# Attention, expert routing and a dense FFN on one core: v as 128 rows, route counts behind the value product, w1 in eight pieces, w2's low products last, a last unit without conditions

## The chip, the core and the metric

The kernel runs on one core of a Trainium2 chip. A core has five engines, each with its own instruction stream: TensorE (PE in the profile, its weight loads PEld), VectorE (DVE), ScalarE (ACT), GpSimd (POOL) and SyncE (SP), which here only issues transfers. The transfers run on 16 DMA engines. The metric is the device time of one execution in microseconds (us); lower is better.

## The reference, cut to what matters

```python
# q, k, v: 8 batches, 8 heads, 576 positions, 64 wide
k_p = k.reshape(B, H, 72, 8, D).mean(axis=3)      # keys and values pooled by 8
v_p = v.reshape(B, H, 72, 8, D).mean(axis=3)
attn = softmax(q @ k_p.T / 8)
x = attn @ v_p                                    # 4608 tokens of 512
do_compute = x @ w_skip > 0                       # other tokens pass unchanged
e = argmax(x @ w_gate)                            # one of 8 experts, 512 -> 1024 -> 512
x = x + gate * (relu(x @ w1[e]) @ w2[e])          # for the tokens that compute
h = x @ w_in                                      # dense FFN, 512 -> 2048 -> 512
out = (h * sigmoid(h)) @ w_out
```

## The kernel before

**Attention** (`attention`, L173 to L418). 36 tiles of 128 tokens run in a software pipeline, i from -2 to 35: in a step PE makes the scores of tile i+2 (`s`, from the key tile `kbd` and `q`), the transposes of tile i+1's weights (`pt`) and the value product of tile i (`pv`, from `pts` and the value tile `vex`). VectorE takes the maxima (`mx`), ScalarE the exponentials (`prb`). The loads of k, q and v (`loadk`, `loadq`, `loadv`) are issued by SP a batch or two ahead, all on one queue. v comes as 120 rows of five chunks (600 places for 8 heads x 72 pooled values). It is pooled by GpSimd and for batch 0 in part by VectorE (L216), then transposed for a small product with the router's weights (`vtp`, `cps`), which fills further columns of `vex`.

**Routing** (`route`, L429). Tokens are routed in groups of 9, 9, 9, 6 and 3 tiles. Each group has steps that are hung between the attention's: `step1` makes a one-hot tile (`rohb`) on VectorE, `count` sums it on PE with two small 0/1 matrices (`trib`, `onesb`; `trib` is cast by `consts`, from the tile `constb`), `step2` makes each token's place (`ix`) on VectorE, and `place` (L529) has GpSimd scatter the tokens' numbers into a list in DRAM (`slots`), one operation of about 1 us per tile. At the end the list is read back as a table.

**Expert units** (`moe`, L794). A unit is up to 384 tokens of one expert. Products are made of three matmuls on parts: each operand is split into a high part (a cast, on ScalarE: `w1h`, `w2h`, `hh`, `xth`) and a low part (the rest, on VectorE: `w1l`, `w2l`, `hl`, `xtl`). `mm1` (L809) makes eight hidden groups f of 12 matmuls each (`hp`, three buffers), high x high, low x high, high x low over four chunks of 128. `mm2` (L847) makes the output for each third s of the unit, 24 matmuls over f (`yp`). `keep` (L805) copies the gathered tokens (`xn`) to `xr` for the residual. The first unit stands ahead of the loop; its weights come during attention (`expert0`, passed to `attention` as `extra`: `conv1` splits w1 chunk by chunk at i = 29 to 32, `xtrans` transposes tokens at i = 34 and 35). Then a `For_i` loop (L947) runs over the units; the hardware loads each unit's token count n and takes one of three versions of `mm1` by nested conditions (L958, L961), and skips thirds (L913). In a pass `second` (L891) has the output products, the scatters of the results to DRAM (which read the token numbers `si`), and the split of the next w1. The last unit stands behind the loop; its matmuls lie inside conditions on its count (L986, L1007), interleaved with the preparation of the FFN's weights.

**The FFN** (`ffn`, from L1105) follows; from about 545 us on it is almost all PE.

**Order.** Every engine runs its instructions in the order of the code (a recording layer, `Ordered`, L110, keeps it, so all these instructions carry line L110); a wait of one holds what stands behind it on its engine.

## Time and profile before

| | us |
|---|---|
| three runs | 1317.8, 1320.7, 1322.06 (median 1320.7) |
| the profiled execution | 1320.69 |
| its span in the trace | 1318.9 |
| PE busy | 1268.2 (96%) |
| VectorE busy | 854.9 (65%) |
| ScalarE busy | 569.1 (43%) |
| GpSimd busy | 354.4 (27%) |

Times in the trace count from the start of the span. The page gives busy shares, and groups of equal instructions with their number, busy time, mean duration and the idle time ahead of them; the timeline gives single instructions (or runs of equal ones, with x and their number) with their start, their duration, and in brackets how long their engine was idle before them and what ended that. A PE row for several matmuls gives the time from the first one's start to the last one's modelled end, so rows overlap a little. The windows view sums a stretch: busy time of each engine, the granted TensorE clock as a share of the full one, the busy share of the DMA engines and the bytes that they moved.

### The profile page before, as it was taken

How to read it: one execution, taken by the hardware profiler on the slowest of the kernel's cores; microseconds unless marked ns; L12 is line 12 of the kernel's file. 1: busy time of each engine (PE TensorE's matmuls, PEld its weight loads, DVE VectorE, ACT ScalarE, POOL GpSimd, SP SyncE). 2: the span in 40 equal slices, each digit the busy share in tenths (PEclk: the TensorE clock that was granted, in tenths of full speed). 3: DMA queues.
4: the chain of work that ended last, by engine and by line, in shares of the span. 5: the costliest groups of instructions: out<-in, count | busy, mean ns of one | idle time of the engine just before them, and what ended most of it. 6: DMA issues, size and time to landing. Idle time of an engine off the chain costs nothing.

```text
span 1318.9 us, 20479 instructions
## 1 busy us (share of the span) xinstructions
PE 1268.2 (96%) x6501; PEld 1081.3 (82%) x6502; DVE 854.9 (65%) x1554; ACT 569.1 (43%) x1188; POOL 354.4 (27%) x312
## 2 busy tenths in 40 slices
PE   5899789999989999999999999999999999999998
PEld 5788778988979888878888888788888888888887
DVE  4677786667667677779833325565784657847565
ACT  4567633454445454344433334433353333533321
POOL 4476332222123230223357603101011110101100
PEclk9999898999999999999999999999999999999999
DMA  9988635555556552248935332635356452463532
GB/s 287 291 261 256 213 132 195 191 188 192 179 197 210 195 191 83 89 160 271 319 115 211 137 121 88 217 126 176 109 189 205 153 175 90 166 203 132 175 107 93
DMA packets 94106, 233.77 MB, mean 177 GB/s; under 512 B 15068, under 2 KB 26972, under 8 KB 90375
## 3 DMA queue, kind: packets, MB, share of 16 engines
q1 hardware_dynamic: 86735, 215.82, 48.9%
q0 software_dynamic: 7008, 16.80, 3.9%
q8 instruction: 42, 0.69, 0.2%
q14 instruction: 33, 0.27, 0.1%
q10 hardware_dynamic: 288, 0.20, 0.1%
HBM read 182.58 MB, written 52.89 MB: 179 GB/s over the span
## 4 chain that ended last, share of the span: by engine, by line
PE 57%; DVE 2%; issue 1%; ACT 1%; DMA 0%; SPq 0%; DVEq 0%; ACTq 0%
PE yb L110 20%; PE ps L110 17%; PE fh L110 9%; PE fop L110 9%; PE yp L110 1%; PE hp L110 1%; DVE ft L110 1%; PE fxp L110 0%; DMA wout<-wdo 0%; DVE fr L110 0%; PE sx L110 0%; DVE fgl L110 0%; DVE fsg L110 0%; ACT fh L110 0%; DVE hl L110 0%
## 5 line engine op out<-in xcount | busy, mean ns | idle before, releaser
L110 PE MATMUL yb<-wout,g 128*128 128x512 f32 x1152 | 268.4, 391 | 0.7 <-DMA wout<-wdo 0.7
L110 PEld LDWEIGHTS yb<-wout,g 128*128 128x128 f32 x1152 | 215.0, 188 | 45.6 <-DMA wout<-wdo 1.1
L110 POOL TENSOR_TENSOR tm<-tm,tm 128x512 f32<-128x512 f32 x24 | 32.3, 1344 | 411.7 <-ACT tm L110 411.7
L110 DVE TENSOR_TENSOR yacc<-yb,yacc 128x512 f32<-128x512 f32 x168 | 116.0, 690 | 38.7 <-PE yb L110 31.4
L110 ACT COPY tm<-ps 128x512 f32<-128x512 f32 x72 | 42.3, 588 | 146.3 <-PE ps L110 144.5
L110 PE MATMUL yp<-w2h,hh 128*128 128x512 f32 x240 | 96.2, 401 | 1.7 <-ACT w2h L110 1.3
L110 PE MATMUL yp<-w2l,hh 128*128 128x512 f32 x240 | 94.3, 393 | 2.4 <-DVE w2l L110 2.4
L110 PE MATMUL yp<-w2h,hl 128*128 128x512 f32 x240 | 94.5, 394 | 0.0
L110 ACT ACTIVATE hh<-hp 128x256 fp32r<-128x256 f32 (+2 forms) x96 | 41.2, 429 | 122.4 <-PE hp L110 113.0
L110 ACT CAST g<-sg 128x512 fp32r<-128x512 f32 x96 | 59.6, 620 | 76.9 <-DVE sg L110 76.9
L110 DVE TENSOR_TENSOR fsg<-fh,fsg 128x512 f32<-128x512 f32 x48 | 33.0, 688 | 81.4 <-ACT fsg L110 81.4
L110 ACT ACTIVATE prb<-s,mx 128x72 f32<-128x72 f32 x288 | 65.2, 343 | 47.4 <-DVE mx L110 46.0
L110 PE MATMUL fh<-w1l,fh 128*128 128x512 f32 x336 | 83.4, 390 | 0.0
L110 DVE TENSOR_TENSOR tm<-ps,tm 128x512 f32<-128x512 f32 x24 | 16.6, 691 | 98.1 <-PE ps L110 98.1
L110 PE MATMUL hp<-xth,w1h 128*128 128x256 f32 (+2 forms) x384 | 72.3, 310 | 5.4 <-PEq L1573 2.3
L110 PE MATMUL hp<-xtl,w1h 128*128 128x256 f32 (+2 forms) x384 | 73.5, 311 | 3.6 <-DVE xtl L110 3.3
L110 DVE SCALAR_TENSOR_TENSOR hl<-hp,hh 128x256 fp32r<-128x256 f32 (+2 forms) x96 | 46.0, 479 | 42.8 <-ACT hh L110 39.5
L110 PEld LDWEIGHTS fh<-w1l,fh 128*128 128x128 f32 x336 | 62.8, 188 | 12.9
L110 PE MATMUL hp<-xth,w1l 128*128 128x256 f32 (+2 forms) x384 | 71.0, 307 | 0.0
L110 DVE TENSOR_TENSOR g<-sg,g 128x512 fp32r<-128x512 f32 x96 | 65.7, 685 | 5.1 <-ACT g L110 4.7
L110 PE MATMUL pv<-vex,pts 120*128 120x148 f32 (+3 forms) x400 | 63.6, 315 | 5.3 <-remote 2.7
L110 DVE TENSOR_TENSOR w2l<-raw,w2h 128x512 fp32r<-128x512 f32 x96 | 65.8, 690 | 3.3
(231 smaller groups left out, 2751.2 us busy)
## 6 DMA issues: line engine op xcount, KB each, us to landing
raw<-w SPq DMA_DIRECT2D x88, 512.0 KB, 3.3
wout<-wdo SPq DMA_DIRECT2D x48, 512.0 KB
win<-wdi SPq DMA_DIRECT2D x36, 512.0 KB
w1l<-wdi SPq DMA_DIRECT2D x36, 512.0 KB
xa<-x SPq DMA_DIRECT2D x36, 256.0 KB
fx<-xa SPq DMA_DIRECT2D x9, 1024.0 KB
v<-vR SPq DMA_DIRECT2D x7, 1200.0 KB
fr<-w_in SPq DMA_DIRECT2D x16, 512.0 KB
```

The source lines that it names most:

```text
L110: ins = f(*a, **k)
```

## The change

The change makes these edits:

- v is padded to 128 rows on the host and loaded as such (two pieces for batch 0, seven whole batches after it). The computation still reads 120.
- k of batch 0 comes in four loads, q's first tile in two, between them; its pooling and key tile are made in matching pieces. The constants are loaded ahead of the identity. For batch 1, q is loaded ahead of v.
- `count` is issued behind the value product of its step; `consts` at i = 8.
- `expert0` splits w1 in eight half chunks (512 columns) at i = 28 to 35; from i = 32 on the low part is made by GpSimd.
- `keep` is one copy on ScalarE.
- In the loop the version of `mm1` for 256 tokens stands first, the one for 384 last.
- `mm2` of the first unit's s = 2 takes the eight products with w2's low part behind the others.
- `si` is made behind the step s = 1 (in the loop that is behind w1's low parts).
- The last unit's count is no longer loaded, and its conditions are gone. (By construction the last unit holds 384 places or none.)

On SP, at the start of the program (`kT`, `qT`, `vR` are the inputs, the numbers behind names count tiles), before:

```order
L110 DMA k_121<-kT 128x1152 x2
L110 DMA q_126<-qT 128x4x128
L110 DMA v_129<-vR 120x1536
L110 DMA v_129<-vR 120x1024
L110 DMA q_126<-qT 128x4x448
L110 DMA wr<-wr 128x144
L110 DMA k_134<-kT 128x2304
L110 DMA v_178<-vR 120x2560
L110 DMA q_180<-qT 128x2304
```

and now:

```order
L110 DMA k_121<-kT 128x576 x2
L110 DMA q_122<-qT 128x2x128
L110 DMA k_121<-kT 128x576 x2
L110 DMA q_122<-qT 128x2x128
L110 DMA v_132<-vR 128x1536
L110 DMA v_132<-vR 128x1024
L110 DMA q_122<-qT 128x4x448
L110 DMA wr<-wr 128x144
L110 DMA k_137<-kT 128x2304
L110 DMA q_185<-qT 128x2304
L110 DMA v_187<-vR 128x2560
```

The k and q pieces alternate, v has 128 rows, and the whole q of batch 1 stands ahead of v.

On PE, near the end of attention, around the count of the fourth group (`rps`), before:

```order
L110 MATMUL pv_2147<-vex_113,pts_2073 128x3x74
L110 MATMUL pv_2147<-vex_113,pts_2073 128x2x74 x3
L110 LDWEIGHTS trib
L110 MATMUL rps_2183<-rohb_2164,trib 128x48
...
L110 MATMUL rps_2183<-rohb_2164,onesb 128x48
...
L110 MATMUL rps_2183<-rohb_2164,onesb 128x8
L110 MATMUL pt_2192<-ident,prb_116 120x128 x3
L110 MATMUL pt_2197<-ident,prb_116 120x128 x2
L110 MATMUL pv_2201<-vex_113,pts_2137 128x2x74
L110 MATMUL pv_2201<-vex_113,pts_2137 128x3x74
L110 MATMUL pv_2201<-vex_113,pts_2137 128x2x74 x3
```

and now:

```order
L110 MATMUL pv_2156<-vex_113,pts_2082 128x3x74
L110 MATMUL pv_2156<-vex_113,pts_2082 128x2x74 x3
L110 MATMUL pt_2195<-ident,prb_116 120x128 x3
L110 MATMUL pt_2200<-ident,prb_116 120x128 x2
L110 MATMUL pv_2204<-vex_113,pts_2146 128x2x74
L110 MATMUL pv_2204<-vex_113,pts_2146 128x3x74
L110 MATMUL pv_2204<-vex_113,pts_2146 128x2x74 x3
L110 LDWEIGHTS trib
L110 MATMUL rps_2210<-rohb_2173,trib 128x48
...
L110 MATMUL rps_2210<-rohb_2173,onesb 128x48
...
L110 MATMUL rps_2210<-rohb_2173,onesb 128x8
```

The count with `trib` and `onesb` has gone behind the transposes `pt` and the value product `pv` that it stood in front of.

On GpSimd, at the end of attention (`xn` is the gather of the first unit's tokens, `ix` the places that a scatter needs), before:

```order
L110 TENSOR_TENSOR vex_113<-vp_1684,consts 120x2x64 x3
L110 DMA slots<-consts,ix_1868 36864x1 x9
L110 DMA xn<-xa,g_85 128x520 x3
L110 DMA slots<-consts,ix_2228 36864x1 x6
L110 MEMSET pad_w_2308 128x1
```

and now:

```order
L110 TENSOR_TENSOR vex_113<-vp_1691,consts 120x2x64 x3
L110 DMA slots<-consts,ix_1875 36864x1 x9
L110 DMA xn<-xa,g_85 128x520 x3
L110 TENSOR_TENSOR w1l<-raw_79,w1h 128x512 x2
L110 DMA slots<-consts,ix_2239 36864x1 x5
L110 TENSOR_TENSOR w1l<-raw_79,w1h 128x512
L110 DMA slots<-consts,ix_2239 36864x1
L110 TENSOR_TENSOR w1l<-raw_79,w1h 128x512
L110 MEMSET pad_w_2323 128x1
L110 DMA slots<-consts,ix_2419 36864x1 x3
```

Four operations for w1's low part stand between the gather and the scatters; the third of them behind five scatters, the fourth behind all six.

The diff, cut to its core:

```diff
@@ loadv, pool_k, keys
-                    nc.sync.dma_start(v_t[b][:CP, c].rearrange("p c t d -> p c (t d)"), self.vR[b][:, c])
+                    nc.sync.dma_start(v_t[b][:, c].rearrange("p c t d -> p c (t d)"), self.vR[b][:, c])
...
+                for a in halves:
+                    eng.tensor_reduce(kp[:, a:a + w], k[:, a:a + w], AX.X, ALU.add)
...
-            def keys(b):
-                kp, kb = st.pop((b, "k")), kbd[b % NB]
-                for j in range(2):
-                    nc.scalar.mul(kb[:, :, j, :], kp, c[:, C_E + j:C_E + j + 1])
+            def keys(b, parts=(slice(4),)):
+                kp, kb = st[b, "k"], kbd[b % NB]
+                for a in parts:
+                    for j in range(2):
+                        nc.scalar.mul(kb[:, a, j, :], kp[:, a], c[:, C_E + j:C_E + j + 1])
@@ attention: start
-            for a in (0, 2):
-                nc.sync.dma_start(k_t[0][:, a:a + 2].rearrange("p a g t -> p a (g t)"), self.kT[0][:, a:a + 2])
+            q_t[0] = s2.tile([P, 4, S], F32, name="q0", tag="q", bufs=3)
+            for a in range(4):
+                nc.sync.dma_start(k_t[0][:, a].rearrange("p g t -> p (g t)"), self.kT[0][:, a])
+                if a % 2:
+                    nc.sync.dma_start(q_t[0][:, a - 1:a + 1, 0:P], self.qT[0][:, a - 1:a + 1, 0:P])
+            nc.scalar.dma_start(c, self.con[:, P:P + C_TRI])
             nc.scalar.dma_start(self.ident, self.con[:, 0:P])
...
-            pool_k(0, nc.vector)
-            keys(0)
+            pool_k(0, nc.vector, range(4), 1)
+            keys(0, (slice(0, 2), slice(2, 4)))
@@ attention: step i
-                if ready and ready[0]:
-                    ready[0]()
                 if i == -2:
                     pool_v(0, ON0)
                     values(0)
+                    loadq(1)
                     loadv(1)
-                    loadq(1)
...
                 if i >= 0:
                     pv(i, pts.pop(i))
+                if ready and ready[0]:
+                    ready[0]()
...
-                if i == 6:
+                if i == 8:
                     self.consts()
@@ conv1, keep
-    def conv1(self, i, eng=None):
-        self.split(self.w1h[:, i], self.w1l[:, i], self.raw1[:, i], eng=eng)
+    def conv1(self, i, eng=None, a=0, m=FM):
+        self.split(*[t[:, i, a:a + m] for t in (self.w1h, self.w1l, self.raw1)], eng=eng)
...
             def keep():
-                nc.scalar.copy(xr[:, U - 1], xn[:, U - 1])
-                nc.vector.tensor_copy(xr[:, 0:U - 1], xn[:, 0:U - 1])
+                nc.scalar.copy(xr.rearrange("p s n -> p (s n)"), xn.rearrange("p s n -> p (s n)"))
@@ mm2
-            def mm2(s, gt, between=None):
+            def mm2(s, gt, between=None, low_last=False):
...
+                a, b, c = (hh, self.w2h), (hh, self.w2l), (hl, self.w2h)
+                order = [(f, t) for f in range(8) for t in (a, b, c)]
+                if low_last:
+                    order = [(f, t) for f in range(8) for t in (a, c)][:-1]
+                    order += [(f, b) for f in range(4)] + [(7, c)] + [(f, b) for f in range(4, 8)]
@@ second
                     if n is None:
-                        mm2(s, gt)
+                        mm2(s, gt, low_last=(s == 2))
...
                     if s == 2:
                         scatter(s)
-                        nc.vector.tensor_scalar(si[:, 0:U - 1], cols[:, 0:U - 1], -1.0, None, ALU.add)
                         if n is not None:
                             self.conv1(0)
...
+                    else:
+                        nc.vector.tensor_scalar(si[:, 0:U - 1], cols[:, 0:U - 1], -1.0, None, ALU.add)
@@ loop
-            nq = nc.value(self.qi[0:1, 1:2], U * P)
...
-                with tc.If(n > 320) as cmp:
-                    mm1(384)
+                with tc.If(n < 257) as cmp:
+                    mm1(256)
                 with cmp.Else():
-                    with tc.If(n > 256) as cmp2:
+                    with tc.If(n < 321) as cmp2:
                         mm1(320)
                     with cmp2.Else():
-                        mm1(256)
+                        mm1(384)
@@ last unit
             for f in range(0, 8, 2):
-                with tc.If(n > 0) as cmp:
-                    nc.before(cmp)
-                    mm1(U * P, (f, f + 1))
-                nc.after(cmp)
+                mm1(U * P, (f, f + 1))
...
             for s in (2, 1):
-                with tc.If(n > P * s) as cmp:
-                    nc.before(cmp)
-                    mm2(s, gt)
-                nc.after(cmp)
+                mm2(s, gt)
@@ host, expert0
+    vr = np.concatenate([vr, np.zeros((B, P - CP, NC, POOL * D), v.dtype)], 1)
...
-                if 29 <= i < 33:
-                    k.conv1(i - 29)
+                if 28 <= i < 36:
+                    k.conv1((i - 28) // 2, k.nc.gpsimd if i >= 32 else None, FM // 2 * (i % 2), FM // 2)
```

## Rows read from the trace of the kernel before

**Rows 1.** of the page: the costliest groups (see the section on the profile), then DMA issues

```profile
L110 POOL TENSOR_TENSOR tm<-tm,tm 128x512 f32<-128x512 f32 x24 | 32.3, 1344 | 411.7 <-ACT tm L110 411.7
...
v<-vR SPq DMA_DIRECT2D x7, 1200.0 KB
```

**Rows 2.** the windows view: window, length, busy us (instructions) of each engine, clock, DMA share, GB/s

```profile
19.00:24.00 5.00, 5.00 (x29) 4.42 (x28) 2.96 (x9) 2.54 (x12) 0.00 (x0) 1.00 1.01 218
25.00:30.00 5.00, 3.83 (x27) 3.21 (x25) 4.79 (x13) 3.41 (x14) 3.99 (x2) 1.00 0.95 390
```

**Rows 3.** the timeline at startup: start, us, engine, operation, [idle before <- releaser]

```profile
8.24 0.96 ACT L110 ACTIVATE kbd<-kp,consts 128x288 f32<-128x288 f32 x2 [5.04 <-DVE kp L110]
...
9.25 2.29 PE L110 MATMUL s<-kbd,q 128*128 128x144 f32 x8 [9.25 <-ACT kbd L110]
...
11.95 2.76 DVE L110 TENSOR_REDUCE vp<-v 120x192 f32<-120x1536 f32 x1
...
14.03 2.06 POOL L110 TENSOR_TENSOR v<-v 120x512 f32<-120x512 f32 x2 [4.19 <-DMA v<-vR]
...
17.13 2.14 PE L110 MATMUL s<-kbd,q 128*128 128x144 f32 x8
...
28.60 1.25 PE L110 MATMUL s<-kbd,q 128*128 128x144 f32 x8 [1.02 <-DMA q<-qT]
```

**Rows 4.** the timeline at 52 to 57 us, ScalarE and TensorE

```profile
52.87 0.30 ACT L110 CAST trib<-constb 128x128 bf16<-128x128 f32 x1 [4.77 <-DMA constb<-con]
...
54.07 1.60 PE L110 MATMUL s<-kbd,q 128*128 128x144 f32 x8 [2.62 <-ACT prb L110]
...
56.44 3.85 PE L110 MATMUL pv<-vex,pts 120*64 120x148 f32 x20
```

**Rows 5.** the timeline at the end of attention

```profile
152.08 3.05 PE L110 MATMUL pv<-vex,pts 120*128 120x148 f32 x10 [2.69 <-remote]
...
162.33 1.30 DVE L110 TENSOR_TENSOR w1l<-raw,w1h 128x1024 fp32r<-128x1024 f32 x1 [0.71 <-ACT w1h L110]
...
165.73 0.18 PE L110 MATMUL rps<-rohb,trib 128*128 128x48 bf16 x1 [2.45 <-DVE rohb L110]
...
170.28 2.51 PE L110 MATMUL pv<-vex,pts 120*64 120x148 f32 x20 [0.91 <-DVE ri L110]
```

**Rows 6.** the timeline around the first unit's first group, GpSimd and TensorE

```profile
172.01 1.02 POOL L110 DMA_INDIRECT slots<-consts,ix  x1 [8.63 <-DVE sc L110]
...
176.37 0.85 PE L110 MATMUL hp<-xth,w1l 128*128 128x384 f32 x4
...
178.50 0.98 POOL L110 DMA_INDIRECT slots<-consts,ix  x1 [0.30 <-issue]
```

**Rows 7.** the timeline in the first unit's second product

```profile
195.80 0.70 DVE L110 COPY xr<-xn 128x1040 f32<-128x1040 f32 x1
...
196.89 2.53 DVE L110 TENSOR_TENSOR w2l<-raw,w2h 128x512 fp32r<-128x512 f32 x4
...
197.62 0.50 PE L110 MATMUL yp<-w2l,hh 128*128 128x512 f32 x1 [1.87 <-DVE w2l L110]
```

**Rows 8.** the timeline of TensorE in the loop's first pass

```profile
219.36 0.39 PE L110 MATMUL hp<-xth,w1h 128*128 128x256 f32 x1 [1.86 <-issue]
...
220.40 1.05 PE L110 MATMUL hp<-xth,w1l 128*128 128x256 f32 x4
...
224.38 0.62 PE L110 MATMUL hp<-xth,w1l 128*128 128x256 f32 x4
```

**Rows 9.** the view of tile hp in 210 to 506 us: forms of ScalarE's relu

```profile
L110 ACT ACTIVATE hh<-hp x80: 383/412/492, 217.3 to 486.1; 128x256 fp32r<-128x256 f32 x40, 128x320 fp32r<-128x320 f32 x32, 128x384 fp32r<-128x384 f32 x8
```

**Rows 10.** the timeline of the pass with the fewest tokens

```profile
385.43 0.17 DVE L110 TENSOR_SCALAR si<-table 128x2 int32 x1 [1.77 <-DMA xa<-x,si]
...
391.17 0.82 PE L110 MATMUL hp<-xtl,w1h 128*128 128x256 f32 x2 [2.39 <-DVE xtl L110]
```

**Rows 11.** the timeline of TensorE at the loop's exit

```profile
505.98 1.34 PE L110 MATMUL hp<-xth,w1h 128*128 128x384 f32 x4 [2.27 <-PEq L1573]
```

More of the change, by code (lines that the diff above doesn't have):

```diff
@@ L200, in loadq, with pool_k @@
                 nc.sync.dma_start(q_t[b], self.qT[b])
-            def pool_k(b, eng, halves=(0, 2)):
+            def pool_k(b, eng, halves=(0, 2), w=2):
                 k = k_t[b]
@@ L206, in pool_k @@
                     kp = s2.tile([P, 4, G], F32, name=f"kp_{b}", tag="kp")
-                if eng is nc.vector:
-                    for a in halves:
-                        eng.tensor_reduce(kp[:, a:a + 2], k[:, a:a + 2], AX.X, ALU.add)
-                else:
-                    eng.tensor_tensor(k[:, :, :, 0:4], k[:, :, :, 0:4], k[:, :, :, 4:8], ALU.add)
-                    eng.tensor_tensor(k[:, :, :, 0:2], k[:, :, :, 0:2], k[:, :, :, 2:4], ALU.add)
-                    eng.tensor_tensor(kp, k[:, :, :, 0], k[:, :, :, 1], ALU.add)
+                for a in halves:
+                    eng.tensor_reduce(kp[:, a:a + w], k[:, a:a + w], AX.X, ALU.add)
                 st[b, "k"] = kp
@@ L769, in moe_first @@
         self.sel, self.nu = [pool.tile([1, 1], I32, name=n, tag=n) for n in ("sel", "nu")]
-        self.qi = pool.tile([1, 2], I32, name="qi", tag="qi")
+        self.qi = pool.tile([1, 1], I32, name="qi", tag="qi")
         sq = pool.tile([P, U + 1], I32, name="sq", tag="sq")
@@ L845, in gates @@
                 return gt
-            def mm2(s, gt, between=None):
+            def mm2(s, gt, between=None, low_last=False):
                 ps = (pp if s else self.hp).tile([P, DM], F32, name=f"yp{s}", tag="yp" if s else "hp")
-                i = 0
-                for f in range(8):
-                    if between and f == 4:
+                a, b, c = (hh, self.w2h), (hh, self.w2l), (hl, self.w2h)
[3 more added lines that the diff above has]
+                    order += [(f, b) for f in range(4)] + [(7, c)] + [(f, b) for f in range(4, 8)]
+                for i, (f, (h, w)) in enumerate(order):
+                    if between and i == 12:
                         between()
-                    for h, w in ((hh, self.w2h), (hh, self.w2l), (hl, self.w2h)):
-                        nc.tensor.matmul(ps, h[:, f, P * s:P * (s + 1)], w[:, f], start=(i == 0), stop=(i == 23))
-                        i += 1
+                    nc.tensor.matmul(ps, h[:, f, P * s:P * (s + 1)], w[:, f], start=(i == 0), stop=(i == 23))
                 nc.vector.scalar_tensor_tensor(y[:, s, 0:DM], ps, gt[:, s:s + 1], xr[:, s, 0:DM], ALU.mult, ALU.add)
@@ L1513, in layout @@
     vr = np.concatenate([vr, np.zeros((B, NC * CP - H * G, POOL * D), v.dtype)], 1)
[L1514 removed]
+    vr = vr.reshape(B, NC, CP, POOL * D).transpose(0, 2, 1, 3)
+    vr = np.concatenate([vr, np.zeros((B, P - CP, NC, POOL * D), v.dtype)], 1)
     wr = np.concatenate([w_gate, w_skip[:, None]], 1).reshape(H, D, E + 1).transpose(1, 0, 2).reshape(D, H * (E + 1))
```

7 lines of the change are left out of this document (removed).

## The prediction

> **What bounds the kernel now.** I read the page first: TensorE (PE) is busy 96% of the span (the table ahead), so in most stages only a change in PE's own work or in its few waits can move the end. I then went through the stretches in order of time and looked in each at the places where PE waits, because the change leaves PE's matmuls as many and as large as they were. The last two thirds (the dense FFN from about 545 us on) hold no edited line; they only shift with their start. So the question is which of PE's waits before that go, and what is late next. The reader should see three kinds of wait in the rows: for loads (startup, and at 54 us), for VectorE or GpSimd work queued in a bad order (166, 197, 391 us), and for the sequencers at the loop's entry and exit (219, 506 us). Behind several of them PE then runs a stretch at the lower of its two clock levels: the 2.62 us wait at 54 us is followed by a value product of 20 matmuls that takes 3.85 us, where the same shape takes 2.51 later [rows 4, 5].
>
> The profiled execution took 1320.69 us, at the median of the three runs (1320.7), so gains are subtracted from it directly. A measurement of this kernel tells about 0.3%, 4 us, from no change.
>
> **Loads of v.** In the stretch 19 to 24 us, which is all v with its 120 rows, the queues are full (share 1.01) and move 218 GB/s; in 25 to 30 us, q and k with 128 rows, they are as full (0.95) and move 390 GB/s [rows 2]. A whole v is 1200 KB [rows 1], 1.23 MB; at 218 GB/s that is 5.6 us. With 128 rows it is 1.31 MB and at the rate of the other loads 3.4 us, so each of the eight loads gets 2.2 us shorter. I take that value since 128 rows is what k and q have; the other end is no gain.
>
> The Trainium skill ("DMA: Bandwidth & Descriptors", "Why a DMA increments its semaphore by 16 and not by 1") says that a transfer goes to the largest number of engines up to 16 that divides its slowest dimension, which is 15 for 120 rows and 16 for 128. By that rule each engine has 8 rows both ways, and v would take as long as before. The row speaks against it as the whole story, since 15 of 16 would cost 6% and the row shows 44% less. What it would give stands among the rivals.
>
> **Startup.** GpSimd waits 4.19 us for v until 14.03, VectorE begins its part of the pooled v at 11.95 and takes 2.76, and the transposes that need both stand ahead of the scores at 17.13 [rows 3]. With v 2.2 to 3 us earlier GpSimd's part comes that much earlier; then VectorE's is the later one. It begins behind the first scores' maxima, and so moves only as far as these. The key tile takes 0.96 us in one piece at 8.24 and the scores 2.29 from 9.25 [rows 3]; in halves, the first half of both (0.5 and 1.1 us) can be done before the second half of k is pooled, which is 1.6 at most. The scores at 17.13 come 1.2 us earlier if the halves bring nothing and 3.1 if both work; I take **2.5**. The constants ahead of the identity and the four smaller k loads I cost at nothing: the same bytes on the same queue.
>
> **q before v.** PE waits 1.02 us at 28.60 for q, which is queued behind v [rows 3]. It is now in front: **1.0**. v(1) is then one load of q later, which at the new rate lands about when it used to; at the old rate its transposes would wait about 2.
>
> **54 us.** ScalarE stands 4.77 us for the small constants, queued behind whole loads, and casts them only at 52.87; the exponentials and PE wait behind it, PE 2.62 [rows 4]. The cast moves two tiles later, and the queues are some 6 us ahead after three faster v. The wait should go, and of the 1.3 us by which the value product behind it was slow about half: **3.2**, bounds 1 and 3.9.
>
> **Count behind the value product, w1 in halves.** At 165.73 PE waits 2.45 for the route's one-hot tile [rows 5]. The work that it stands in front of (transposes of the next weights) could not have begun much earlier, because VectorE did 1.30 us of w1's low part at 162.33 ahead of the maxima. In the new order that piece is on GpSimd, and the count comes after the value product. I take **2.0** for this place; at the other three counts the wait was far shorter. VectorE's route steps behind a count start later by a value product, and so do the scatters of slots; GpSimd is idle 8.63 us before them [rows 6]. The 2.69 us wait at 152.08 [rows 5] is for value tiles which VectorE made late for a reason that I can't see in the trace; I count nothing for it, and 2.7 as the upper end.
>
> **The price: w1's low parts on GpSimd.** The third and fourth chunk's low parts now stand in GpSimd's queue among the slot scatters. The first half of the fourth chunk stands behind five scatters that wait for the route's index. Those start at 172.01 and follow each other at 1.30 us, so the fifth is over at 172.01 + 4 x 1.30 + 1.0 = 178.2; a GpSimd operation of 128 x 512 takes 1.34 us [rows 1]. The piece is there at about 179.8. The first unit's first group of matmuls needs it in its last product, the fourth of those at 176.37, so at 176.9 [rows 6]. PE stands 2.9 us. Since slow matmuls follow several of PE's longer waits [rows 4, 8, 11], I charge **-3.5**. Bounds: 0 (the index comes earlier because VectorE has less to do) and -4.6 (the wait and a whole slow stretch of 1.7, as at the loop's entry below). The second half, behind one more scatter, is needed four groups later and is covered.
>
> **First unit's second product.** PE waits 1.87 us at 197.62 for w2's low parts 4 to 7, which VectorE makes from 196.89 in 2.53 us [rows 7]. With the low products last, PE has 19 products that need none of them; the copy of xr (0.70 us) no longer stands ahead of them on VectorE [rows 7], so the last is there at 196.89 + 2.53 - 0.70 = 198.7, and the product can't end sooner. The wait goes; some of it may come back for the very last part, or a slow stretch behind it may go too: bounds 1.0 and 2.9, **1.8**.
>
> **Loop entry.** In the first pass PE stops 1.86 us at 219.36 with nothing to wait for that the trace shows, in the second group of the 256-token branch, which stands last in the code; the matmuls after it run at 1.05 us for four instead of 0.62 further on [rows 8]. In the four later passes of that size the row isn't there. I read it as the jump over the two longer branches while the weights of the pass are loading. With the 256 branch first the code runs on. Gain 0 to 3.6 (1.86 and four groups at 0.43 more): **1.9**.
>
> **si behind w1's low parts.** In the pass of fewest tokens VectorE waits 1.77 us at 385.43 until a scatter has read si, ahead of w1's four low parts, and PE waits 2.39 at 391.17 for what follows them [rows 10]. si moves behind: **1.7**; the rest of the 2.39 stays with the low parts themselves. Elsewhere in the loop it costs nothing, since the scatter that reads si is not waited for by PE.
>
> **xr in one copy.** VectorE's copy of two thirds takes 0.70 us [rows 7]; ScalarE's of the whole I put at up to 2, and it must now wait for VectorE's last read of xr. The first relu of a pass is some 1 us later then. The cover is the matmuls' three output buffers, that is two groups of three such rows as the 0.62 us one [rows 8]. So 0, and -2 if the cover fails in some passes.
>
> **Last unit without conditions.** The matmul at 505.98 waits 2.27 us at the loop's exit, and its four take 1.34 us, where four of this shape take 0.85 [rows 6, 11]. The barrier stays; a load of the count to a register and eight pairs of branches go. **1.2**, between 0.5 and 2.5.
>
> **Sum:** 2.5 + 1.0 + 3.2 + 2.0 - 3.5 + 1.8 + 1.9 + 1.7 + 1.2 = 11.8 us; 1320.7 - 11.8 = **1308.9 us**.
>
> **Rivals.** *v stays slow.* If what holds the rate is not the 120 rows (the rule above), startup gives 1 instead of 2.5, q before v loses 2 at v's transposes instead of 0, and of the 3.2 at 54 us half stays: 1.5 + 2 + 1.6 less, 1314 us. For it: the number of engines differs only by one. Against: in the rows two full queues differ by 390 to 218. *More than counted.* The wait at 152 us goes with the lighter VectorE (2.7), the slow stretches go with the waits before them, and GpSimd's pieces come in time: 8 more, 1301 us.
>
> *Slower.* The stop at 219 us may be the price of every jump past code that has not been fetched, and the new order would then move it behind the branch: the 256-token passes jump past two blocks at the end of theirs, the 320-token passes past one. The rows count five passes of 256 (40 groups of 8), four of 320 and one of 384 [rows 9]. Each stop costs 1.86 and a slow stretch of 1.7, some 3.5 us. Without the gain of 1.9 the kernel stands at 1310.8; four stops make 1324.8, from there on it is slower, and nine make 1342. Against it: in the present code later passes jump too, over 384 and 320 to the 256 branch, and don't stop; that is why I hold it for unlikely. If only the first pass stops, 1314.
>
> **How the numbers follow.** Forecast with its bounds, 1303 to 1313: 0.60. v stays slow: 0.12. One first stop, or GpSimd's price at its bound, 1313 to 1318: 0.10. More than counted: 0.13. Jumps: 0.05. The range takes in the first three and the better case down to 2 us beyond its value, and leaves out the jumps and the far ends: 1299 to 1318. Faster by over 0.3% (below 1316.7): the forecast, the better case, nearly all of the slow v and of the one stop, 0.60 + 0.13 + 0.10 + 0.04 = 0.87, less 0.02 for several costs at once: 0.85. Slower (above 1324.7), the jumps: 0.05. Within: 0.10.
>
> **What would show it.** Right: v windows at about 390 GB/s; scores (1) near 14.5; no wait near 51 us; no 2.45 us wait for the one-hot tile; a PE wait of about 3 us in the first unit's first group whose releaser is GpSimd's low part; no 1.87 wait for w2's low parts; no stop in the first pass. Wrong: v still near 218 GB/s, or "issue" waits on PE behind the branch in many passes, or a first-unit wait far above 5 us because the route's index came late.

## The result and the profile after

The changed kernel takes 1329.6 us (median of six runs, 1328.1 to 1331.9) against 1321.4 of the kernel before beside it: 1.0066 times as long, 95% interval 1.0045 to 1.0086. The forecast was 1308.9. The profiled execution's span is 1329.8 us (before 1318.9), and PE is busy 1272.4 us in it, 4 us more than before: the rest is waiting. In the experiments one execution, of run 12, took 7194 us where the other three took 1304.9 to 1307.5; it is left out.

To see where the time went, I compared the start of every PE matmul in the two traces. Negative numbers are us that the changed kernel is ahead of the one before, at that time of the old trace:

| time before | place | ahead (-) or behind (+) |
|---|---|---|
| 17 | end of the startup | -0.75 |
| 60 | behind the constants' cast | -5.5 |
| 107 | behind two counts | -1.5 |
| 160 | end of attention's tiles | +1.0 |
| 173, 181 | first unit's first groups | +3.7, +6.1 |
| 201 | first unit's second product | +3.1 |
| 215, 223 | loop, first and second groups | +8.8, +5.3 |
| 243 | loop, behind the first pass | +12.1 |
| 388, 394 | pass of fewest tokens | +13.0, +10.5 |
| 415 | the same, its end | +14.4 |
| 525 to the end | last unit, dense FFN | +11.1 |

So PE gains at 54 us, in the second product, at the loop's entry, in the pass of fewest tokens and at the last unit, and five stretches lose more than all that: 60 to 160, 160 to 181, 201 to 215, 223 to 243 and 394 to 415. The waits view of the changed kernel (engine, tile, releaser; us in total, times, longest) names most of them:

```profile
PE pv L110 <- DVE x L110: 7.6, 8, 2.8
PE xtp L110 <- DVE xtl L110: 6.2, 2, 3.3
PE pv L110 <- DVE vex L110: 4.3, 1, 4.3
...
PE xtp L110 <- issue: 3.2, 1, 3.2
PE hp L110 <- POOL w1l L110: 2.4, 1, 2.4
```

Only the last of these was in the prediction's sum. Two of the others stood in part in the kernel before, which waits 2.69 us for the same `pv` [rows 5] and 2.71 for one of the two `xtp`.

**Loads.** The windows view (columns as in [rows 2]) of the whole v and of the loads behind it:

```profile
18.00:23.00 5.00, 5.00 (x28) 4.42 (x27) 3.02 (x10) 2.45 (x11) 0.00 (x0) 1.00 1.01 424
24.00:28.00 4.00, 3.32 (x25) 2.89 (x23) 3.90 (x11) 2.40 (x10) 3.58 (x2) 1.00 1.00 420
```

128 rows take v from the 218 GB/s of [rows 2] to 424. Run 4 below, the kernel before with this part alone, shows the same in a stretch that is all v:

```profile
16.00:18.50 2.50, 2.50 (x12) 2.21 (x10) 0.91 (x2) 1.54 (x8) 0.64 (x2) 1.00 1.00 422
```

By the rule that the prediction quoted from the Trainium skill ("DMA: Bandwidth & Descriptors", "Why a DMA increments its semaphore by 16 and not by 1") an estimated 6% of the rate was to be had; the measurement decides, it was nearly a factor of two. The DMA view counts 66 packets of some 10 KB in 20 to 23 us of the kernel before, with the engines full, which is 0.74 us for each; in 20 to 22 us of the changed one 83 of them, 0.39 us each. Why a packet takes longer with 120 rows, no run shows. What the faster v did at startup stands in the timeline (start, us, engine, operation, [idle before <- releaser]), to be held against [rows 3]:

```profile
11.38 2.78 DVE L110 TENSOR_REDUCE vp<-v 120x192 f32<-120x1536 f32 x1 [0.23 <-DMA v<-vR]
...
13.28 2.06 POOL L110 TENSOR_TENSOR v<-v 120x512 f32<-120x512 f32 x2 [6.23 <-DMA v<-vR]
...
16.38 1.90 PE L110 MATMUL s<-kbd,q 128*128 128x144 f32 x7
```

GpSimd still waits for v, until 13.28 instead of 14.03. Run 4 below shows what the faster v alone does there.

**Counts.** VectorE and PE at the first count:

```profile
63.15 0.16 DVE L110 TENSOR_TENSOR tot<-tot,rps 128x8 f32<-128x8 f32 x1 [1.21 <-PE rps L110]
...
64.71 0.17 DVE L110 SCALAR_TENSOR_TENSOR ix<-pf,sl 128x9 int32<-128x9 f32 x1
64.80 0.16 DVE L110 TENSOR_SCALAR sm<-pv 128x8 f32<-128x8 f32 x1
...
66.11 1.66 PE L110 MATMUL pv<-vex,pts 120*128 120x148 f32 x10 [0.79 <-DVE x L110]
```

VectorE waits 1.21 us for the count (`rps`), which now comes behind the value product. It then does the nine route steps from `tot` to `ix`, and only after them the sums `sm` and the outputs `x` of the tile before, for which PE's next value product waits. This place costs 1.2 us, the next two counts 1.1 and 1.3. The other 2.8 us or so that are lost between 60 and 141 us go at two places without a count, where VectorE stands still for no reason that I found (see "Still open" below).

**GpSimd's pieces.** GpSimd, VectorE and PE in the last group's route and at the first unit's first group (timeline):

```profile
164.06 0.20 DVE L110 TENSOR_REDUCE rm<-req 128x6 f32<-128x48 f32 x1
164.30 1.88 DVE L110 TENSOR_TENSOR roh<-req,rm 128x48 f32<-128x48 f32 x1
...
164.82 2.60 POOL L110 TENSOR_TENSOR w1l<-raw,w1h 128x512 fp32r<-128x512 f32 x2
...
166.21 1.27 DVE L110 TENSOR_TENSOR rohb<-roh,rdo 128x48 bf16<-128x48 f32 x1
...
168.89 3.05 PE L110 MATMUL pv<-vex,pts 120*128 120x148 f32 x10 [2.79 <-DVE x L110]
...
181.51 1.28 POOL L110 TENSOR_TENSOR w1l<-raw,w1h 128x512 fp32r<-128x512 f32 x1
...
182.85 0.44 PE L110 MATMUL hp<-xth,w1l 128*128 128x384 f32 x1 [2.45 <-POOL w1l L110]
```

The two VectorE steps `roh` and `rohb` end with GpSimd's two pieces, at about 166.1 and 167.4. They last 1.88 and 1.27 us; without GpSimd beside them such steps take 0.21 (run 13 below). PE's next value product waits 2.79 us for what follows on VectorE. The Trainium skill ("GPSIMD Engine Reference", "1. Specifications") says that GpSimd shares its ways to SBUF with VectorE, and that VectorE's instructions with two SBUF inputs contend for them. The trace agrees and gives the price here: such a step lasts until the GpSimd instruction beside it ends. A step with one input from SBUF isn't slowed: VectorE's pooling of k takes 1.34 us beside GpSimd's work on v,

```profile
24.34 4.53 POOL L110 TENSOR_TENSOR v<-v 120x1280 f32<-120x1280 f32 x2 [6.58 <-DMA v<-vR]
...
25.11 1.34 DVE L110 TENSOR_REDUCE kp<-k 128x144 f32<-128x1152 f32 x1
```

and 1.34 us at 20.71 with GpSimd idle. Of the rows ahead of these, the last two are the wait that was predicted.

**Loop.** The timeline of PE at the end of the first pass's branch:

```profile
235.74 0.39 PE L110 MATMUL hp<-xth,w1l 128*128 128x256 f32 x2
239.38 1.51 PE L110 MATMUL xtp<-ident,xn 128*128 128x128 f32 x6 [3.25 <-issue]
241.32 0.79 PE L110 MATMUL yp<-w2h,hh 128*128 128x512 f32 x1 [0.43 <-PEq L909]
...
245.81 0.58 PE L110 MATMUL yp<-w2l,hh 128*128 128x512 f32 x1
246.22 0.40 PE L110 MATMUL yp<-w2h,hl 128*128 128x512 f32 x1
```

The windows view of that stretch (the clock stands ahead of DMA share and GB/s), and then the DMA view's row for the instruction queue in 236.0 to 236.5 us (packets, MB, share):

```profile
239.00:246.00 7.00, 6.20 (x17) 4.76 (x18) 3.84 (x11) 4.22 (x7) 1.86 (x2) 0.53 0.41 142
```

This row, of another view, is the packet:

```profile
q8 instruction: 1, 0.02, 11.3%
```

The stop of [rows 8] in the second group is gone. One of 3.25 us stands at the end of the branch, and behind it PE runs at the lower clock level (1.2 GHz; 0.53 of the full clock as the mean of 239 to 246 us) until 246.2, with 0.58 to 0.63 us for a matmul that then takes 0.40. A packet of code arrives at the start of the stop; what the rest of the 3.25 us is, the trace doesn't show. Between 250 and 520 us, in all later passes, this queue brings no packet and PE has no such stop. The Trainium skill ("Runtime: NRT & Kernel Launch", "Instruction fetch mechanics") says that a taken branch to code that is not at hand must wait for a fetch; the trace agrees for the first pass, as far as this packet goes.

**Second product.** The wait of [rows 7] is gone, and PE gains 3.0 us between 181 and 201. No run has this part alone, and run 4 speaks against it: its products stand in the old order, it has the same wait,

```profile
189.37 0.50 PE L110 MATMUL yp<-w2l,hh 128*128 128x512 f32 x1 [1.87 <-DVE w2l L110]
```

and yet by the same comparison it gains 2.3 us on the kernel before over the whole product (190 to 203 us of the old time), where run 7, with the low products last, gains 2.0. What the kernel before lost there is mostly a stretch at the lower clock level behind the wait, which run 4 doesn't have. The windows of the two, before and run 4 (clock ahead of DMA share and GB/s):

```profile
199.10:202.50 3.40, 3.40 (x9) 2.61 (x8) 2.59 (x15) 0.72 (x2) 1.01 (x2) 0.51 0.77 201
189.90:193.00 3.10, 3.10 (x15) 2.50 (x14) 2.77 (x12) 0.00 (x0) 1.97 (x2) 1.00 0.62 176
```

### The profile page after: what moved, and what is told of

It is laid out like the page before. It is cut to its first block, busy times and chain, and to the rows that moved or that the text cites. A ratio compares the mean times of both kernels' runs of the same rounds, so it can differ in the third digit from the quotient of the medians.

```text
span 1329.8 us, 20559 instructions
## 1 busy us (share of the span) xinstructions
PE 1272.4 (96%) x6501; PEld 1082.6 (81%) x6502; DVE 844.0 (63%) x1543; ACT 579.5 (44%) x1194; POOL 357.0 (27%) x316
## 4 chain that ended last, share of the span: by engine, by line
PE 56%; DVE 3%; ACT 1%; issue 1%; POOL 0%; DMA 0%; DVEq 0%; ACTq 0%; POOLq 0%
PE yb L110 20%; PE ps L110 16%; PE fh L110 9%; PE fop L110 9%; PE yp L110 1%; DVE fr L110 1%; DVE ft L110 1%; PE fxp L110 0%; DVE raw L110 0%; PE sx L110 0%; DVE fgl L110 0%; DVE fsg L110 0%; DVE w2l L110 0%; ACT g L110 0%; PE hp L110 0%
## 5 line engine op out<-in xcount | busy, mean ns | idle before, releaser
L110 PE MATMUL yp<-w2h,hh 128*128 128x512 f32 x240 | 99.0, 413 | 1.7 <-PEq L909 0.4
L110 PEld LDWEIGHTS pv<-vex,pts 120*128 120x128 f32 (+1 forms) x400 | 57.0, 187 | 17.5 <-issue 9.1
L110 POOL DMA_INDIRECT xn<-xa,gi x33 | 38.4, 1162 | 108.5 <-PE hp L110 81.3
```

The lines of the kernel that those rows point to most:

```text
L110: ins = f(*a, **k)
```

## The experiments

There are eighteen runs, of thirteen kernels, in five sets, each set on one chip beside runs of the kernel before; the ratios are to those. The numbers of the runs are the ones that the expectations use. Ratios of one set can be compared closely; between sets one kernel's ratio moved from 0.9946 to 0.9924 (runs 7 and 13), which is 3 us.

**Set 1: which part carries the loss?** Run 1 puts the count back, run 2 takes the pieces off GpSimd, run 3 puts count and w1's four pieces back, run 4 is the kernel before with 128 rows of v.

```
run 1:  the two lines `if ready and ready[0]: ready[0]()` ahead of ptrans again
run 2: -  k.conv1((i - 28) // 2, k.nc.gpsimd if i >= 32 else None, ...)
       +  k.conv1((i - 28) // 2, None, FM // 2 * (i % 2), FM // 2)
run 3:  run 1, and
       -  if 28 <= i < 36: k.conv1((i - 28) // 2, ...)
       +  if 29 <= i < 33: k.conv1(i - 29)
run 4 (before): -  v_t[b][:CP, c] ...     +  v_t[b][:, c] ...   (and vR padded)
```

> The changed kernel with one part undone: the four route counts stand ahead of the transposes and the value product again. Theory A (the count behind the value product is the main loss: VectorE makes its route steps then in front of the next tile's sums, and TensorE waits for these): 5 to 7 us less than the changed kernel's 1329.6, so 1323 to 1325, and TensorE's waits for x of 0.8 to 1.4 us after each count are gone. Theory B (w1's low parts on GpSimd are the main loss): at most 1 us less.

> The changed kernel with w1's eight half pieces as they are, but all low parts on VectorE, none on GpSimd. Theory B (GpSimd's pieces make VectorE's small operations beside them slow, hold the slot scatters, and through these the table and the loop's first gather): 5 to 8 us less than 1329.6, so 1322 to 1325; the 2.8 us wait for x at 169 us and the 2.4 us wait for GpSimd's low part at 181 us are gone. Theory A: 0 to 2 us less.

> The changed kernel with both undone: counts ahead, w1 in four whole pieces on VectorE at the old steps. If A and B together are the loss: 11 to 14 us less than 1329.6, so 1316 to 1319, faster than the kernel before. If the loss lies elsewhere (loop, loads): above 1322.

> The kernel before with one part alone: v loaded as 128 rows. Both theories: the v stretches move 400 GB/s or more instead of 218, the 2.62 us wait at 54 us goes with its slow stretch, startup gains under 1 us: 3 to 5 us less than the kernel before, about 1317. Rival C (the faster loads only get in the way of stores and instruction fetches): no gain, or slower.

Measured: run 1 1326.2 us, 1.0076 (1.0048 to 1.0105); run 2 1320.2, 1.0032 (1.0020 to 1.0044); run 3 1323.1, 1.0050 (1.0031 to 1.0069); run 4 1314.2, 0.9980 (0.9963 to 0.9997). Taking GpSimd out saves about 4 us by the ratios. Putting the count ahead alone (run 1) shows no clear gain (1.0076, the changed kernel 1.0066 and in run 5 1.0090), where theory A had 5 to 7 us, and run 3 with the count ahead is even slower than run 2 with it behind, from which it differs by w1's halves too. With both suspects out (run 3) the kernel is still slower than before. In run 3's trace PE is 12.8 us ahead of the old trace at 223 us and only 5.3 ahead at 243: the loop's first pass takes 7.5. Run 4 came out 2 us faster than the kernel before, where 3 to 5 were expected, but in its trace the wait at 54 us is gone, though the constants are cast in the old step:

```profile
46.45 0.38 ACT L110 CAST trib<-constb 128x128 bf16<-128x128 f32 x1
```

It gains 4.6 us there, and the changed kernel, whose constants come later too, 4.65: that gain is the faster v's. Run 4 also gains 1.8 us at startup; its GpSimd gets v at 10.88, 3.2 us earlier than before:

```profile
10.88 2.07 POOL L110 TENSOR_TENSOR v<-v 120x512 f32<-120x512 f32 x2 [1.19 <-DMA v<-vR]
...
15.33 2.14 PE L110 MATMUL s<-kbd,q 128*128 128x144 f32 x8
```

In the changed kernel the same piece lands at 13.28. Ahead of it on SP's queue k and q now come in six smaller loads instead of three, and on ScalarE's queue the constants have changed places. Together this takes back 2.4 us of v, and 1.05 of the 1.8 us at the scores; no run tells the two apart.

**Set 2: the order of the branches and the copy.** Run 5 is the changed kernel again; run 6 is run 3 with 384 first and 256 last; run 7 also has xr copied by both engines; run 8 is run 2 with both edits.

```
runs 6 to 8: -  with tc.If(n < 257) as cmp: mm1(256)
             +  with tc.If(n > 320) as cmp: mm1(384)        (and so on, as before)
runs 7, 8:   -  nc.scalar.copy(xr..., xn...)
             +  nc.scalar.copy(xr[:, U - 1], xn[:, U - 1])
             +  nc.vector.tensor_copy(xr[:, 0:U - 1], xn[:, 0:U - 1])
```

> The changed kernel itself, unaltered, so that the next three stand beside it on one chip. Both theories: 0.5 to 0.8% slower than the kernel before, PE's one stop with no releaser (about 3.2 us) in the first pass ahead of the identity transposes, with a slow stretch behind it.

> The changed kernel with the count ahead of the value product, w1 in four whole pieces on VectorE, and the order of the branches put back (384 first, 256 last). The third kernel had all but the last and was 0.50% slower. Theory A, the jump past unfetched code behind the 256 branch costs more than the one ahead of it: in the third kernel's trace the loop entry gains 3.6 us and the stop of 4.3 us with its slow stretch then loses 7.4, so this one is 3 to 4 us faster than the third, 0.2 to 0.3% slower than before. Theory B, the stop comes with something else of the change (the copy of xr on ScalarE, the place of si) or the next wait takes what it gives back: within 1 us of the third, 0.45 to 0.55% slower.

> The run before this, with xr copied by ScalarE and VectorE as in the kernel before, too. What is left of the change: 128 rows of v, the startup order with halves, q before v, constants two tiles later, w2's low products last, si behind, the last unit without conditions. Theory A, the copy on ScalarE delays the gather by the 1 to 2 us that PE then waits for xn: 1 to 4 us faster than the run before, level with the kernel before or up to 0.3% faster. Theory B, the gathers are late because PE comes earlier: within 1 us of the run before.

> The changed kernel with w1's pieces all on VectorE (as the second run, 0.32% slower), the order of the branches and the copy of xr put back; the count stays behind the value product. Theory A: 4 to 7 us faster than the second run, 0 to 0.2% faster than before, and no gap to the run before this one, which differs in the count's place and w1's pieces alone. Theory C, the count behind the value product costs the 3 us that the traces of the second and third run show between 60 and 142 us: 3 us slower than the run before this one.

Measured: run 5 1330.2, 1.0090 (1.0065 to 1.0116); run 6 1316.5, 0.9985 (0.9970 to 1.0000); run 7 1311.0, 0.9946 (0.9924 to 0.9968); run 8 1316.5, 0.9985 (0.9969 to 1.0001). Run 7 beats both kernels: before by 0.5%, the changed one by 19 us in one set. The copy costs 5.5 us (run 6 to 7), more than I expected. Run 8 is 5.5 us above run 7: theory C, the count costs too. How the copy loses shows in the pass of fewest tokens. ScalarE waits there for VectorE's last read of xr (the first row), copies for 1.50 us, and only then can GpSimd begin the gather into `xn`. In run 6:

```profile
383.14 0.74 DVE L110 SCALAR_TENSOR_TENSOR x<-yp,gt,xr 128x512 f32<-128x512 f32 x1
...
384.22 1.50 ACT L110 COPY xr<-xn 128x1560 f32<-128x1560 f32 x1 [3.90 <-DVE x L110]
...
386.72 1.44 POOL L110 DMA_INDIRECT xn<-xa,gi  x1 [5.29 <-PE hp L110]
...
395.11 0.66 PE L110 MATMUL xtp<-ident,xn 128*128 128x128 f32 x4 [0.81 <-DMA xn<-xa,gi]
```

and in run 7, where PE has no such wait:

```profile
383.25 0.74 DVE L110 SCALAR_TENSOR_TENSOR x<-yp,gt,xr 128x512 f32<-128x512 f32 x1
...
384.08 0.70 DVE L110 COPY xr<-xn 128x1040 f32<-128x1040 f32 x1
...
385.75 1.55 POOL L110 DMA_INDIRECT xn<-xa,gi  x1 [5.28 <-PE hp L110]
```

At the first unit the copy gains nothing either. The timeline of PE there in run 6:

```profile
205.39 1.01 PE L110 MATMUL xtp<-ident,xn 128*128 128x128 f32 x6 [2.71 <-DVE xtl L110]
```

and in run 7:

```profile
204.54 1.01 PE L110 MATMUL xtp<-ident,xn 128*128 128x128 f32 x6 [0.99 <-DVE xtl L110]
```

Without the 0.70 us copy VectorE and PE come 0.9 us earlier, but the gather's third part ends later and the work behind it is 0.85 us later: the gain turns into a wait of 2.71 us, with slow matmuls behind it. Why that gather ends later isn't shown, since the copy is over long before it. In the changed kernel's pass of fewest tokens PE waits twice for the gather, 2.1 us in all. Of run 6's loss 3 us fall at 640 us, in the FFN, where ScalarE waits for an input; run 3's trace has 2.2 us there and run 7's nothing. It is hardly the copy: the changed kernel and run 5, which have the copy too, lose nothing there, and run 8, which hasn't, loses 1.8 us between 530 and 620. So of the 3.9 us between the two traces about 1 can be read from rows as the copy's, and the rest of the 5.5 us between the times is open.

**Set 3: single parts on run 7.** Run 9 puts the 256 branch first again, run 10 the count behind, run 11 `si` ahead of w1's low parts; run 12 has the 256 branch between the others:

```
run 12: with tc.If(n > 320): mm1(384)   else: with tc.If(n < 257): mm1(256)   else: mm1(320)
```

> The seventh run (0.54% faster than before), with one thing of the change put in again: the 256 branch first. Theory A, the end of that branch now jumps over two blocks not yet fetched: PE stops 3 to 4.5 us ahead of the identity transposes in the first pass and runs a slow stretch behind, against a stop of 2.1 us in the branch that goes away: 4 to 7 us slower than the seventh run, level with before or up to 0.1% faster. Theory B, the 8 us between the third and the sixth run were two chips' difference: within 1.5 us of the seventh run.

> The seventh run with the count behind the value product put in again, w1's four pieces whole and on VectorE. Theory C, VectorE's route steps then stand between a value product and the sums of the next tile, and PE waits 0.8 to 1.5 us with each count of the first three groups: 4 to 6 us slower than the seventh run, with PE 5 to 6 us late at 155 us. Theory D, the gap between the seventh and eighth run comes from w1's halves: within 1.5 us of the seventh run.

> The seventh run with si put back ahead of w1's low parts. As in the prediction: 1.7 us slower than the seventh run, PE's wait for the transposes' low parts in the pass of fewest tokens back from 1.3 to 2.4 us or more. Rival: the low parts alone set that wait, no difference.

> The seventh run with the 256 branch between the two others: 384 first, then 256, then 320. The first pass then jumps over one block ahead of its matmuls and over one behind them. Theory A (each jump over unfetched code stops PE unless matmuls queued ahead cover it): a stop of 1 to 2.5 us in or ahead of the branch and one of 3 us or more behind it, 3 to 7 us slower than the seventh run. Theory E (the price grows with the code jumped over): the two stops add up to about what one jump over two blocks costs, between the seventh and the first run of this set.

Measured: run 9 1310.7, 0.9968 (0.9955 to 0.9981); run 10 1309.3, 0.9959 (0.9947 to 0.9971); run 11 1309.3, 0.9957 (0.9940 to 0.9973); run 12 1305.9 (median of three), 0.9934 (0.9913 to 0.9954). Run 9's trace follows theory A: it wins 3.8 us at the loop's entry and loses 8.7 behind the branch. Run 12 wins 3.6 and loses 3.9. With `si` put back (run 11) PE loses 1.5 us in its pass against run 7, but not in a longer wait (1.20 us for the low parts against 1.28): the matmuls ahead of that wait ran slower. The times can't tell it. Against run 7, in another set, these differences came out smaller than in set 2, and so the next set has run 7 in it.

**Set 4: single parts beside run 7.** Run 13 is run 7; run 14 adds the eight pieces with GpSimd; run 15 is run 9; run 16 is run 10.

> The seventh kernel again (the change without the count's new place, w1's pieces, the order of the branches and the one copy of xr), so that single additions stand beside it on one chip. Expected: 0.4 to 0.6% faster than before.

> The same with w1 in eight half pieces, the last four on GpSimd. Theory A (two prices: VectorE's small route operations run beside GpSimd's pieces five times longer, and the slots behind the pieces delay the table and the first gather): 3 to 5 us slower than the run before, PE late both at 169 and at 181 us. Rival, the price is the prediction's, the wait of 2.4 us in the first unit alone, and part of it comes back behind: 0 to 2 us slower.

> The same with the 256 branch first. By the third against the sixth run 8 us slower, by the ninth against the seventh 3, by the trace of the ninth 5 at the loop's first pass. Expected: 3 to 5 us slower than the first run of this set; 8 would say that the stop differs by what stands ahead of it.

> The same with the count behind the value product, w1 whole. By the eighth against the seventh run 5 us slower, by the tenth 1.5. In the traces of one set VectorE stands some 3 us with nothing to wait for at three places with the count behind and at one with the count ahead, in those of the other set at none. Theory C: 3.5 to 4 us slower in the counts; 5 to 6 where the stalls are there, and 3 or less at the end where they are not.

| run | us | ratio to before | against run 13 |
|---|---|---|---|
| 13 base | 1309.9 | 0.9924 (0.9909 to 0.9940) | |
| 14 GpSimd's pieces | 1317.0 | 0.9978 (0.9963 to 0.9993) | +7.1 us |
| 15 256 first | 1315.7 | 0.9968 (0.9952 to 0.9983) | +5.9 us |
| 16 count behind | 1315.0 | 0.9965 (0.9952 to 0.9978) | +5.1 us |

Run 14 shows both of GpSimd's prices, on VectorE and on PE (timeline):

```profile
157.70 1.59 DVE L110 TENSOR_TENSOR req<-lg,rmx 128x48 f32<-128x48 f32 x1
...
160.37 1.18 DVE L110 TENSOR_TENSOR sb<-sb,rdo 128x6 f32<-128x6 f32 x1
...
175.90 0.44 PE L110 MATMUL hp<-xth,w1l 128*128 128x384 f32 x1 [2.56 <-POOL w1l L110]
```

In run 13 the same two steps take 0.21 and 0.17:

```profile
157.97 0.21 DVE L110 TENSOR_TENSOR req<-lg,rmx 128x48 f32<-128x48 f32 x1
...
159.25 0.17 DVE L110 TENSOR_TENSOR sb<-sb,rdo 128x6 f32<-128x6 f32 x1
```

Against run 13, PE in run 14 is 2.9 us late at 167, 7.2 at 174 and 9.0 at 208, where the first gather has come late (first part at 196.88 instead of 190.11). Of this 3.3 come back at the loop's entry, whose stop shrinks from 2.64 to 0.94. Run 15's stops are longer than run 13's single one and there are two of them:

```profile
224.38 1.51 PE L110 MATMUL xtp<-ident,xn 128*128 128x128 f32 x6 [3.35 <-issue]
...
228.93 0.80 PE L110 MATMUL yp<-w2h,hl 128*128 128x512 f32 x1 [1.32 <-issue]
```

Run 16 settles the 2.45 us of [rows 5]. The wait for the one-hot tile is gone, and in its place PE waits for ScalarE's copy of the weights:

```profile
165.79 0.88 PE L110 MATMUL pt<-ident,prb 128*120 128x128 f32 x5 [2.96 <-ACT pts L110]
```

**Set 5: a jump, or the code jumped over?** Run 17 is run 7, run 18 is run 12.

> The seventh kernel once more, as the reference for the next run on one chip: 0.4 to 0.8% faster than before.

> The same with the 256 branch between the other two. Theory E (the price of a jump grows with the code jumped over): one block ahead costs nothing and one behind about 4 us, against 3.6 us for two blocks ahead, so level with the run before within 1.5 us. Rival, by the twelfth run's time against the seventh's in another set: 1.5 us or more faster.

Measured: run 17 1310.6, 0.9934 (0.9922 to 0.9946); run 18 1310.1, 0.9929 (0.9917 to 0.9942). Level, as theory E had it, though by another way: the 4 us that theory E put behind the branch aren't in run 18's trace, which loses 1.4 there. In run 18 the first pass stops neither in the branch nor at its end, only 0.87 us later:

```profile
223.55 0.50 PE L110 MATMUL yp<-w2h,hl 128*128 128x512 f32 x1 [0.87 <-issue]
```

By the traces PE stops for less with one block on each side than with two ahead (0.87 against 2.52 us in run 17); by the times the two are level, and two behind are 5.9 us slower (run 15). The stop isn't paid by jump.

## Why the prediction was wrong

Four steps of the prediction failed: the count's (nothing urgent was thought to stand behind the moved steps), GpSimd's (its price was one wait on PE), the loop entry's ("with the 256 branch first the code runs on") and the copy's (put at 0). Between runs of one set that differ by one of them alone they cost 5.1, 7.1, 5.9 and 5.5 us, where the sum had a gain of 0.4 for all four.

The measured column takes the matmul comparison of the changed kernel's trace where a place stands alone, and the single-part runs (times) for the four parts that they undid.

| term | predicted | measured |
|---|---|---|
| startup | 2.5 | 0.75 |
| q before v | 1.0 | 0 |
| 54 us | 3.2 | 4.75 (4.6 of it in run 4 too) |
| count, w1 in halves | 2.0 | -5.1 (run 16) |
| GpSimd's pieces | -3.5 | -7.1 (run 14) |
| first unit's second product | 1.8 | 3.0 (not shown to be the edit's) |
| loop entry | 1.9 | -5.9 (run 15) |
| si | 1.7 | 1.5 in its pass (run 11) |
| xr in one copy | 0 | -5.5 (runs 6, 7) |
| last unit | 1.2 | 2.0 |

The measured terms sum to -11.6, and by the ratios the changed kernel came out 8.7 (first measurement) and 11.9 us (run 5) slower than before. That they meet is in part luck: the column mixes traces with times, and singly the parts overlap. The four bad ones sum to 23.6 us, where runs 5 and 7 differ by 19.2.

**What held.** v at full rate, and in run 4 3.2 us earlier (in the changed kernel 0.75); the wait at 54 us gone, with more of the slow stretch than the half I took, but through v and not, as I had it, through the cast's new step too; GpSimd's wait (2.45 us, predicted 2.9); the wait for w2's low parts gone, though run 4 gains as much in that product with the wait in place; `si`'s size in its pass; the last unit (the text's eight pairs of branches are six conditions in the code).

**Startup.** The step "the four smaller k loads I cost at nothing: the same bytes on the same queue" failed, as far as run 4 can tell: with the old loads the faster v is there 2.4 us sooner. PE's wait for q is gone as planned, but in its place PE waits 0.68 us at 27.51 for the key tile (`kbd`), and so the term of 1.0 brought nothing.

**Count.** Two steps failed. "VectorE's route steps behind a count start later by a value product" was followed only to the scatters, which have slack. I didn't ask what stands behind those steps on VectorE: the next tile's sums, which PE waits for. Also, the 2.45 us were counted as gone although the text itself says that the transposes could not have begun much earlier; run 16 shows that wait at 2.96 with another releaser. The price of the count is not a fixed one: set 1 (runs 1, 2 and 3) shows no clear one.

**GpSimd.** The price counted the position in GpSimd's queue alone. Missing were the VectorE steps that wait out a GpSimd instruction, and the chain of slots, table and gather behind the pieces, which the first unit's end then waits for.

**Loop entry.** The jump as the cause of the stop was right; the step "with the 256 branch first the code runs on" failed, because the end of that branch now jumps past the two other blocks. "If only the first pass stops, 1314" was the true rival, priced at a gain lost and one stop of 3.5. It cost 6.5 to 9.5 us behind the branch, since a slow stretch of 7 us follows the stop [the 239.38 to 246.2 rows above], against 3.6 to 4.4 won at the entry. The many jumps that I feared didn't stop: later passes fetch no code.

**xr.** "ScalarE's of the whole I put at up to 2" was right (1.50 us), and so was the cover of the relu. I looked only at the relu; the gather into xn waits for the copy as well, and PE for the gather. In run 6 the gather begins 2.84 us behind the end of VectorE's last read of xr, in run 7 1.76. That is the step that failed; it explains about 1 of the 5.5 us.

**The chances.** 0.05 for slower was far too little. I gave the parts' bounds as if each were a known quantity with a sign, while three of the moved instructions (count, GpSimd's pieces, the copy) had a consumer behind them that I hadn't looked at.

**Still open.** In the traces before and after, and in all of sets 2, 4 and 5, VectorE stands 2.2 to 3.7 us ahead of the same `sm` near the end of attention though the value product that it reads is long done. Before it was a part of what stood behind the 2.69 us of [rows 5]; in run 13 it reads (timeline of VectorE):

```profile
143.72 0.17 DVE L110 TENSOR_SCALAR sm<-pv 128x8 f32<-128x8 f32 x1 [3.40 <-PE pt L110]
```

The kernels of these sets with the count behind have three such places. No trace of sets 1 and 3 has one, and the kernel before is 3 us or more faster there (1316.2 and 1314.8 us, otherwise 1319.3 to 1321.4). Sets 3 and 4 ran on one and the same chip, so it is neither the kernel nor the chip alone. No instruction packet falls into these stalls, and I found no releaser. They make the count dearer: 0.25% or 3.3 us without them (run 10 against run 12 in set 3, run 12 being level with run 7 by set 5), 5.1 with them in set 4.

## What to carry to other kernels

When an instruction is moved back, follow everything that is queued behind it on every engine that consumes it, not only the one consumer that had slack. A piece of work that is given to an idle GpSimd can still slow VectorE's small steps with two SBUF inputs many times over, so it belongs where VectorE has nothing urgent. Padding loads to 128 rows nearly doubled their rate here, and done alone it made the kernel 0.2% faster (run 4). Once the four costly parts were undone, what was left of the change (128 rows, the startup order, constants later, w2's low products last, `si` behind, no conditions in the last unit) made a kernel 0.5 to 0.8% faster than before; of these only 128 rows ran alone and only `si` was put back singly (run 11), and neither the constants nor the low products are shown to bring anything of that. A gain in one place must also be followed to the next wait: in the changed kernel the 3 us of the second product were lost again at the end of the first unit.

## What the runs showed of the hardware

- A load of 120 rows moved 218 GB/s at full queues and one of 128 rows 422 to 424; a packet of some 10 KB took 0.74 us in the one and 0.39 in the other.
- VectorE steps with two SBUF inputs that last 0.17 to 0.21 us took 1.18 to 1.98 beside a GpSimd instruction of 128x512, and ended with it; a step with one SBUF input took 1.34 us with and without GpSimd beside it.
- The first pass through a loop paid for code that a jump skipped to: one stop of 0.9 to 1.7 us with one block on either side, 0.7 to 2.6 with two ahead, and 3.2 to 4.6 with two behind, in some runs with a second one of 1.2 to 1.3. In the changed kernel's later passes PE stopped nowhere so, and no code was fetched.
- After such a stop of 3.25 us the matmuls ran about 7 us at the lower clock level, which cost about as much as the stop (6.8 us lost between 223 and 243).
